# First attention layer of a two-layer hybrid model: the division of two softmaxes moved to TensorE and ScalarE, eight copies split by channel, one layer's order rewritten

## The chip, the core and the metric

One core of a Trainium2 chip runs the whole program in one launch. The metric is device time in microseconds. Engines are named as in the profile: PE (TensorE: matmuls and transposes into PSUM), DVE (VectorE), ACT (ScalarE), POOL (GpSimd) and SP (SyncE); the last two issue DMAs here. PSUM has eight banks, each as large as one 128 x 512 tile of 32-bit numbers.

## The reference, cut to what matters

Two kinds of layer alternate, A B A B, on `x` of 2048 tokens and 512 channels, each applied to the row-normalized `x` and added to it.

```
x = x + A(layernorm(x))     # long convolution: FFT, times the spectrum of K, inverse FFT; K from A, B, C, dt
x = x + B(layernorm(x))     # attention, 32 heads of 16, each token sees 8 keys at distances 0, 2, ... 14
x = x + A(layernorm(x))
x = x + B(layernorm(x))

def B(x):
    q, k, v = split(x @ wqkv)
    logits = q . k[pos - off] * scale         # masked where pos - off < 0
    attn = softmax(logits, over the 8 keys)
    o = sum over the 8 keys of attn * v[pos - off]
    return o @ wo
```

The softmax divides by its sum: exp(s (l - max)) / sum.

## The kernel before, in words

The convolution kernel's spectrum is made first (`kgen`), together with the first convolution. Then come the first attention layer, the second convolution (`a_layer`, order `CONV2`) and the second attention layer. Everything stays on the chip; the 16 token rows of a partition are grouped by four (`g` 0 to 3), so `Xg[g]` is 128 x 4 x 512.

An attention layer is written by `b_layer`. It registers small operations with a `Plan`: the engine (or a choice of engines, with an estimated time for each), the function that issues it, what it waits for, and which PSUM buffer it takes and drops. The text `LAYERS[layer]["order"]` then gives the order in which they are issued. A word names an operation: a block (for example `S20`), and a letter for its place in the block. A `+` behind a word takes the second engine of the choice (DVE, where the choice is ACT or DVE). Every engine works through its own instructions in that order. Times in the plan serve only to place filler matmuls on PE (`stream`); nothing in the finished program is scheduled by them.

The blocks of the layer are:

- `y0` to `y3`: last stage of the convolution before (PE), copied to `Xg` by ACT (L1532). `n0` to `n3`: statistics of a row (L1158, L1161, DVE), their logarithm and exponential (ACT), and the normalized row (L1174 on DVE or L1172 on ACT). `t0` to `t3`: transposes, copied by ACT and DVE (L1191).
- `K`, `Q`, `V`: projections (PE, L1205 and L1292), copied by ACT (L1208, L1299).
- `M0`, `M1`: nine DMAs each inside the value tile `V2` (L1316), that build the shifted copies; SP issues five, POOL four. They wait for all eight value copies of their half of the heads.
- `L`: products of queries with shifted keys (DVE, L1253 and L1255), summed by PE, copied to `Lsb` by ACT (L1280).
- `S i jh`: softmax of head group `i` (0 to 3) and half `jh` of the rows. Three DVE instructions find the maximum (L1336, L1342, L1344; one PE swap between them). For groups 0 and 1 DVE subtracts it (L1347) and ACT takes the exponential (L1348); for groups 2 and 3 (`pe_max`) PE subtracts it in PSUM and ACT takes the exponential from there (L1358). PE sums (L1369), ACT takes the logarithm of the sum (L1378) and the exponential of its negative (L1379, 128 columns), and DVE multiplies by it (L1380).
- `P`: attention times values (DVE, L1401), summed by PE (L1411), copied to `oT` by ACT (L1422).
- `R0` to `Rf`: output projection of one row plus `x` (PE, L1441, L1446), copied to `Xg` by ACT (L1469), for nine rows with a running sum for the next mean.
- `N0` to `N3`: normalization of the new `x`, and first stage of the next convolution. Each row gives two tiles, cosine (`r` = 0, from the pool `psA` of four banks) and sine (`r` = 1, from `psL` of two banks), and each tile is copied into `Z` by ACT or DVE (L1489). All 32 copies wait for `X`, the point at which the memory of queries and keys is free.

The second convolution starts with `T0` (L248): PE transposes of the first eight groups of channels in `Z`, into a bank of the space that `psA` had. A DVE copy (L254), a matmul (L263) and an ACT copy (L269) follow, and so on for sixteen such slices, each of which needs its own sixteenth of the channels from all 32 copies.

The functions that the change touches and what calls them:

Of the kernel before, what the change touches and what calls it, by code (L numbers as in the profile page):

```python
# [14 lines left out]
F32 = mybir.dt.float32  # L15
# [14 lines left out]
GE = 4  # L30
# [830 lines left out]
class Plan:  # L861
# [44 lines left out]
    def run(self, order):  # L906
# [16 lines left out]
        if todo:  # L923
# [15 lines left out]
    dict(order="y0a y0b y0c y0d n0a n0b n0c n0e n0d n0h n0g n0i n0f y3a y3b n3a n3c y1a y1b n3b n1a n0j n0k y1c y1d n1b n0l n0p+ n0o+ n0m+ n0n "  # L939
# [40 lines left out]
         third_norm=(),  # L980
         raw=[],
         y_add=[],
         pe_den=(),
         ot_any=[],
         thirds=[],
         stores=[]),
# [36 lines left out]
         kept=[],  # L1023
         third_norm=(),
         raw=[],
         y_add=[],
         pe_den=(),
         ot_any=[],
         thirds=[12, 13, 14, 15, 10, 11],
# [675 lines left out]
```

## Time and profile before

| what | value |
|---|---|
| timed runs | 423.75, 425.57, 426.43 us, median 425.57 |
| profiled execution | 423.79 us, its span 422.0 us |
| PE clock granted | 0.999 |
| DVE busy in the span | 399.5 us, 95% |
| ACT busy in the span | 329.4 us, 78% |
| first attention layer | 151 to 275.2 us of the span |
| second convolution, sixteen slices | 275.2 to some 303 us |
| second attention layer | from 303 us to the end |

In the tables by stretch, a row gives the stretch, its length, then busy time and count of instructions of PE, PE weight loads, DVE, ACT and POOL, the granted clock, the share of DMA time and GB/s. In the tables of groups, a row gives the code line, engine, operation, output and input with shapes and count, then the busy time of the group and the mean of one in ns, then the engine's idle time just ahead of the group and what ended it. In a timeline, start and length in us come first, and idle time stands in brackets.

### The profile page before, as it was taken

How to read it: one execution, taken by the hardware profiler on the slowest of the kernel's cores; microseconds unless marked ns; L12 is line 12 of the kernel's file. 1: busy time of each engine (PE TensorE's matmuls, PEld its weight loads, DVE VectorE, ACT ScalarE, POOL GpSimd, SP SyncE). 2: the span in 40 equal slices, each digit the busy share in tenths (PEclk: the TensorE clock that was granted, in tenths of full speed). 3: DMA queues.
4: the chain of work that ended last, by engine and by line, in shares of the span. 5: the costliest groups of instructions: out<-in, count | busy, mean ns of one | idle time of the engine just before them, and what ended most of it. 6: DMA issues, size and time to landing. Idle time of an engine off the chain costs nothing.

```text
span 422.0 us, 12184 instructions
## 1 busy us (share of the span) xinstructions
PE 373.6 (89%) x5071; PEld 257.2 (61%) x5112; DVE 399.5 (95%) x736; ACT 329.4 (78%) x598; POOL 26.0 (6%) x68
## 2 busy tenths in 40 slices
PE   1167998999989999999997899889999999996996
PEld 1033685676458755687865565368855686875563
DVE  5999999999889989899999999999989999999994
ACT  6999999998979989757655489989988676663542
POOL 5000011011210000002010000000000001200000
PEclk9999999999999999999999999999999999999999
DMA  8900001253889950006282062239300009360022
GB/s 239 427 28 0 3 13 46 76 167 102 253 245 273 275 193 3 2 2 123 55 168 59 2 196 57 99 102 294 109 0 4 2 2 168 63 124 2 26 78 101
DMA packets 25823, 44.09 MB, mean 104 GB/s; under 512 B 7318, under 2 KB 17239, under 8 KB 25127
## 3 DMA queue, kind: packets, MB, share of 16 engines
q1 hardware_dynamic: 22918, 38.09, 31.4%
q0 software_dynamic: 1888, 4.56, 5.0%
q8 instruction: 40, 0.66, 0.7%
q10 hardware_dynamic: 960, 0.66, 0.5%
q14 instruction: 17, 0.13, 0.1%
HBM read 29.04 MB, written 6.95 MB: 85 GB/s over the span
## 4 chain that ended last, share of the span: by engine, by line
PE 39%; DVE 27%; ACT 11%; issue 6%; DMA 5%; SPq 2%; DVEq 0%; ACTq 0%
DVE prodpv L1401 11%; PE ps_qk L1205 8%; DVE prodqk L1255 5%; PE vp L291 4%; PE ps_v L1292 4%; PE psg L601 3%; PE Lp L1277 3%; ACT Z L1489 2%; DVE Z L504 2%; PE psk L568 2%; DMA Kt<-kt_scratch 2%; DMA V<-V 2%; PE ps_y L344 2%; PE pt_x L1188 2%; ACT xc L269 2%
## 5 line engine op out<-in xcount | busy, mean ns | idle before, releaser
L1401 DVE TENSOR_TENSOR prodpv<-V,Lsb 128x2048 bf16<-128x2048 bf16 x64 | 75.3, 1218 | 0.1
L1205 PE MATMUL ps_qk<-xnT,wqk 128*128 128x512 bf16 x256 | 60.1, 379 | 0.0
L1253 DVE TENSOR_TENSOR prodqk<-qT,N 128x1024 bf16<-128x1024 bf16 (+3 forms) x88 | 42.5, 538 | 2.1 <-ACT N L1208 1.8
L1255 DVE TENSOR_TENSOR prodqk<-qT,N 128x1024 bf16<-128x1024 bf16 (+3 forms) x56 | 40.5, 762 | 0.2 <-ACT qT L1208 0.2
L1411 PEld LDWEIGHTS <-prodpv 128*128 128x128 bf16 x1024 | 34.3, 98 | 9.8 <-DVE prodpv L1401 4.1
L1411 PE MATMUL po<-halves,prodpv 128*128 128x64 bf16 x1024 | 37.3, 193 | 2.9 <-DVE prodpv L1401 2.9
L275 DVE TENSOR_TENSOR pab<-xc,Kt 128x2048 bf16<-128x2048 bf16 (+1 forms) x34 | 38.6, 1151 | 0.1
L1205 PEld LDWEIGHTS <-wqk 128*128 128x128 bf16 x256 | 23.6, 98 | 23.5 <-DVE xnT L1191 0.2
L269 ACT CAST xc<-xp 128x1024 bf16<-128x1024 f32 (+1 forms) x34 | 34.7, 1035 | 2.1 <-PE xp L263 1.2
L291 PEld LDWEIGHTS <-pab 128*128 128x128 bf16 x512 | 30.4, 98 | 6.3 <-DVE pab L275 2.8
L291 PE MATMUL vp<-sb_IC,pab 128*128 128x128 bf16 x512 | 33.3, 219 | 0.9 <-ACT VT L295 0.4
L295 ACT CAST VT<-vp 128x1024 bf16<-128x1024 f32 (+1 forms) x31 | 32.5, 1079 | 0.2 <-PE vp L291 0.2
L1441 PE MATMUL ps_o<-wo_t,oT 128*128 128x512 bf16 x122 | 31.9, 379 | 0.6
L1422 ACT CAST oT<-po 128x512 bf16<-128x512 f32 x32 | 17.7, 588 | 18.5 <-PE po L1411 18.4
L1277 PEld LDWEIGHTS <-prodqk 128*128 128x128 bf16 x1024 | 29.3, 96 | 4.5 <-DVE prodqk L1255 1.8
L1277 PE MATMUL Lp<-sb_bones,prodqk 128*128 128x8 bf16 x1024 | 30.2, 166 | 1.2 <-DVE prodqk L1255 1.1
L1292 PE MATMUL ps_v<-wv,xnT 128*128 128x256 bf16 x256 | 30.3, 272 | 0.0
L528 PE MATMUL psadd<-Z,sb_ident 128*128 128x512 bf16 (+3 forms) x72 | 18.5, 339 | 12.9 <-DVE Z L504 6.9
L1299 ACT CAST V<-ps_v 128x512 bf16<-128x512 f32 x32 | 18.6, 585 | 13.2 <-PE ps_v L1292 13.1
L1158 DVE BATCH_NORM_STATS2 ln_stats<-X 128x6 f32<-128x512 bf16 x39 | 24.8, 679 | 2.8 <-ACT X L1532 2.7
L1208 ACT CAST N<-ps_qk 128x512 bf16<-128x512 f32 x32 | 18.5, 590 | 10.5 <-PE ps_qk L1205 10.2
L1292 PEld LDWEIGHTS <-xnT 128*128 128x128 bf16 x256 | 24.3, 97 | 3.6
(197 smaller groups left out, 821.7 us busy)
## 6 DMA issues: line engine op xcount, KB each, us to landing
Kt<-kt_scratch SPq DMA_DIRECT2D x60, 256.0 KB
kt_scratch<-ks SPq DMA_DIRECT2D x32, 128.0 KB
G<-c_G SPq DMA_DIRECT2D x2, 1536.0 KB
V<-V SPq DMA_DIRECT2D x8, 288.0 KB
X<-in_A_u_dram SPq DMA_DIRECT2D x4, 512.0 KB
F1Tsb<-c_F1T SPq DMA_DIRECT2D x2, 1024.0 KB
V<-V SPq DMA_DIRECT2D x4, 512.0 KB
V<-V POOLq DMA_DIRECT2D x4, 384.0 KB, 8.3
```

What stands on the lines that cost most here:

```text
L269: nc.scalar.copy(xcs[cg][:, gs].rearrange("q g o l -> q (g o l)"), xps[cg][:].rearrange("q h n -> q (h n)")[:, gs.start * 128:gs.stop * 128])
L275: nc.vector.tensor_tensor(pabs[cg][:, gs], xcs[cg][:, gs].to_broadcast([128, gs.stop - gs.start, 2, 128]), kts[cg][:, gs], ALU.mult)
L291: a.last_pe = nc.tensor.matmul(vp[:, g, :], pabs[cg][:, gs.start + g, ab, :], C["IC"][:, ab, :], start=(ab == 0), stop=(ab == 1))
L295: copy(dst[..., parts(cg)[part]], vps.pop((cg, part))[:].rearrange("k g (q e) -> k q e g", e=GE))
L1205: nc.tensor.matmul(t.ps[:], wqk[:, ct, f0:f0 + 128], x_group(g)[:, :, ct], start=(ct == 0), stop=(ct == 3))
L1253: nc.vector.tensor_tensor(b.pr[:, u:u + 2 * n, 1 - halves_of[0], :], q, cols(kT[i][:, starts[0]:starts[0] + n * 128]), ALU.mult)
L1255: nc.vector.tensor_tensor(b.pr[:, u:u + 2 * n].rearrange("f u a q -> f a u q")[:, ::-1], q.unsqueeze(1).to_broadcast([128, 2, 2 * n, 64]), ...
L1277: nc.tensor.matmul(t.Lp[:, w, u % 2, u // 2, :], b.pr[:, u].rearrange("f a q -> f (a q)"), bones[:], start=False, stop=(t.parts == W // 2 ...
L1292: nc.tensor.matmul(t.ps[:, jj, :], tokens(ct, jp * 2 + jj, c), wv[:, ct, fp * 256:(fp + 1) * 256], start=(jj + ct == 0), stop=(jj == 1 and ...
L1401: nc.vector.tensor_tensor(t.p2[:, c:c + k, 0:nj, :].rearrange("p c j (d h) -> p c j d h", d=DH), m.V2[i // 2][:, c0 + c:c0 + c + k, r0:r0 ...
L1411: nc.tensor.matmul(po[jj // k][:, jj % k, c, :], t.p2[:, c - c0, jj, :], fold, start=(first and c == c0 and jj % k == 0), stop=(last and c ...
L1441: nc.tensor.matmul(t["ps"][:], m.oT[:, ft, j * 128:(j + 1) * 128], wo_t[:, ft, :], start=(start and ft == lo), stop=(ft == 3 or kept and f ...
```

## The change

In the first attention layer only:

1. `pe_den=(2, 3)`: for head groups 2 and 3 the first exponential goes to a tile of its own; ACT makes only the logarithm of the sum; PE builds the difference again, now with the logarithm subtracted as a third matmul; and a second exponential of 512 columns on ACT writes the finished weights. The multiply on DVE (L1380) and the 128-wide exponential (L1379) go, for four softmaxes.
2. `z_split`: for rows 8 to 11 (the group `N2`) each of the eight copies into `Z` becomes two, one for channels 0 to 255 and one for 256 to 511, each on either engine. The sine tiles of these rows are taken from `psO` (two banks) instead of `psL`.
3. The copy of an output row can go to DVE where no running sum is wanted.
4. A block `C` of operations that issue nothing stands for the first slice of the next convolution: its first step needs only the first halves, later ones the second halves as well.
5. A new order of the whole layer.

Counted by words and their marks, the new order differs from the old as follows (first attention layer, before and after):

| kind | DVE | ACT |
|---|---|---|
| normalized rows | 30 to 27 | 2 to 5 |
| whole copies into `Z` | 10 to 5 | 22 to 19 |
| halves: first, second | 0 to 4, 0 to 3 | 0 to 4, 0 to 5 |
| output rows | 0 to 2 (rows 11, 12) | 16 to 14 |
| softmax multiply, groups 2 and 3 | 4 to 0 | |

Three of the eight split tiles have one half on each engine. Behind the last first half stand two second halves on DVE and three on ACT. SP's moves of `M0` go in the order (numbers from 0) 2, 4, 6, 0, 8 instead of 0, 8, 4, 6, 2; number 0 is the largest. The first values used are those of head group 1 (`P10`) instead of group 0 (`P00`). Memory that the copies need is free (`X`) at word 526 of 734 instead of 552 of 713.

```diff
 LAYERS = (
-    dict(order="y0a y0b y0c y0d n0a n0b n0c n0e n0d n0h n0g n0i n0f y3a y3b n3a n3c y1a y1b n3b n1a n0j n0k y1c y1d n1b n0l n0p+ n0o+ n0m+ n0n "
...
-               "N2m N3m+ N3q N3r N3t N3w N1p N3E N3u N2n+ N2p+ N2C N2q+ N2o+ N3s+ N2A N2E N2y N2w N2s N2D N2G N2z+ N2x+ N2t+ N2F N2B N2H N2u N2v "
-               "N2r",
+    dict(order="y0a y0b y0c y0d n0a n0b n0c n0e n0d n0i n0f y1a y1b n1a n0h n0g y1c y1d n1b n1c y2a y3a n0j n0k y2b y3c n2a n1d n0l n1e n0p+ "
...
+               "N3B N3t N3C N3w N3s N3D N3u N2n+ N2s N3F N2q+ N2p+ N2o+ N2Q N2M N2t+ N2N+ N2O+ N3G+ N2I N2w N2u N3E N2A N2r N2P N2B+ N2y N2x N2z "
+               "N2R N2U N2V N2J N2v N2E N2F+ N2S+ N2W Ca Cb N2C+ N2K N2G Cc Cd Ce N2D N2X N2H N2L N2T",
...
-         pe_den=(),
+         z_split=[[8, 0], [8, 1], [9, 0], [9, 1], [10, 0], [10, 1], [11, 0], [11, 1]],
+         pe_den=(2, 3),
...
-            got["X", j] = plan.add("ACT", act_us(512) + 0.095 * (j % 4 in x_sums[j // 4] and not last_layer), evict, [p], drop=[alloc])
+            if j % 4 in x_sums[j // 4]:
+                got["X", j] = plan.add("ACT", act_us(512) + 0.095, evict, [p], drop=[alloc])
+                return
+            got["X", j] = plan.add(dict(ACT=act_us(512), DVE=0.61), None, evict, [p], drop=[alloc])
+
+        firsts, seconds = [], []
...
-                        t.ps = (m.psL if r else psA).tile([128, 512], F32, name="ps_s", tag="psL" if r else "psA")
+                        t.ps = dict(psA=psA, psL=m.psL, psO=m.psO)[t.pool].tile([128, 512], F32, name="ps_s", tag=t.pool)
...
-                    def evict(eng, jj=jj, r=r, t=t):
+                    def evict(eng, c0=0, c1=16, jj=jj, r=r, t=t):
                         (nc.scalar.copy if eng == "ACT" else nc.vector.tensor_copy)(
-                            z_view(m.Z)[:, r, 4 * g + jj], t.ps[:].rearrange("k (c e g) -> k c g e", c=16, e=GE))
-                    p = plan.add("PE", 0.22, pe, [normed[jj]], take=PL if r else PA)
-                    plan.add(dict(ACT=act_us(512), DVE=0.61), None, evict, [p, x_end], drop=[p])
+                            z_view(m.Z)[:, r, 4 * g + jj, c0:c1], t.ps[:, c0 * 32:c1 * 32].rearrange("k (c e g) -> k c g e", c=c1 - c0, e=GE))
+                    split = [4 * g + jj, r] in lay["z_split"]
+                    pool = PA if not r else PO if split else PL
+                    t.pool = pool[0]
+                    p = plan.add("PE", 0.22, pe, [normed[jj]], take=pool)
+                    if not split:
+                        firsts.append(plan.add(dict(ACT=act_us(512), DVE=0.61), None, evict, [p, x_end], drop=[p]))
+                        continue
+                    us = dict(ACT=act_us(256), DVE=0.34)
+                    halves_of = [plan.add(us, None, lambda eng, c0=c0, evict=evict: evict(eng, c0, c0 + 8), [p, x_end]) for c0 in (0, 8)]
+                    firsts.append(halves_of[0])
+                    seconds.append(halves_of[1])
+                    plan.add("-", 0.0, lambda: None, halves_of, drop=[p])
...
+        if not last_layer:
+            plan.block = "C"
+            p = plan.add("PE", 0.44, lambda: None, firsts, take=PA, cols=0)
+            plan.add("-", 0.0, lambda: None, [p], drop=[p])
+            o = plan.add("DVE", 0.6, lambda: None, [p] + seconds)
+            p = plan.add("PE", 0.43, lambda: None, [o], cols=0)
+            plan.add("ACT", 0.905, lambda: None, [p] + seconds)
```

More of the change, by code (lines that the diff above doesn't have):

```diff
@@ L1026 @@
          y_add=[],
+         z_split=[],
          pe_den=(),
```

50 rows, old and new, of the table LAYERS are left out of this document.

## The prediction

> **What bounds the kernel now.** I read the page first, then busy time by stage, then what VectorE (DVE) waited for, then the timeline around the end of the stage that the change rewrites. The page gives the span and the busiest engine:
>
> ```profile
> span 422.0 us, 12184 instructions
> PE 373.6 (89%) x5071; PEld 257.2 (61%) x5112; DVE 399.5 (95%) x736; ACT 329.4 (78%) x598; POOL 26.0 (6%) x68
> ```
>
> The whole change lies in the first attention layer, from 151 us (first output rows of the first convolution) to 275.2 us (last copy into `Z`). By stretch (columns: PE, weight loads, DVE, ACT, POOL):
>
> ```profile
> 151.00:275.20 124.20, 116.96 (x1570) 76.67 (x1576) 120.58 (x241) 91.26 (x197) 4.44 (x8) 1.00 0.28 71
> 215.00:235.00 20.00, 16.88 (x351) 12.54 (x352) 20.00 (x29) 10.42 (x24) 0.00 (x0) 1.00 0.43 93
> 235.00:255.00 20.00, 18.35 (x306) 12.22 (x308) 20.00 (x30) 14.91 (x42) 0.00 (x0) 1.00 0.35 107
> 255.00:275.20 20.20, 17.84 (x130) 8.02 (x130) 19.54 (x44) 20.07 (x50) 0.00 (x0) 1.00 0.24 79
> 240.50:275.20 34.70, 31.76 (x363) 17.29 (x364) 34.04 (x67) 33.04 (x87) 0.00 (x0) 1.00 0.34 107
> ```
>
> DVE works 120.58 of 124.20 us, so it idles 3.6 us, all of it near the two ends: from 215 to 255 it is full. In the last 20 us ACT is full too (20.07 of 20.20). DVE is the bound, and at the end DVE and ACT are bounds together. What DVE waited for in this stage and in the next convolution:
>
> ```profile
> DVE ln_stats L1158 <- ACT X L1532: 1.4, 1, 1.4
> DVE zt L254 <- PE pt L248: 1.1, 2, 0.8
> DVE prodqk L1253 <- ACT N L1208: 0.9, 1, 0.9
> DVE ln_nb L1166 <- ACT ln_rstd L1165: 0.6, 1, 0.6
> ```
>
> The border itself, by the timeline:
>
> ```profile
> 270.72 4.50 ACT L1489 CAST Z<-ps_s 128x512 bf16<-128x512 f32 x9
> ...
> 270.97 1.70 DVE L1174 TENSOR_SCALAR N<-X,ln_rstd,ln_nb 128x512 bf16<-128x512 bf16 x5
> ...
> 272.58 2.54 DVE L1489 CAST Z<-ps_s 128x512 bf16<-128x512 f32 x4
> ...
> 275.27 0.90 PEld L248 LDWEIGHTS <-Z 128*128 128x128 bf16 x16 [1.64 <-ACT Z L1489]
> ...
> 275.94 0.69 DVE L254 COPY zt<-pt 128x1024 bf16<-128x1024 bf16 x1 [0.81 <-PE pt L248]
> ```
>
> Both engines finish their copies at about 275.2; only then does PE transpose, and DVE stands 0.81 us. That hole is what the channel halves can fill.
>
> **The change part by part.** Prices are distances from start to start where operations follow each other, since they overlap by some 0.04 to 0.1 us. The rows:
>
> ```profile
> L1380 DVE TENSOR_TENSOR Lsb<-Lsb,sm_rdb 128x512 bf16<-128x512 bf16 x16 | 6.6, 417 | 0.0
> L538 ACT CAST Utab<-psadd 128x512 bf16<-128x512 f32 x8 | 4.5, 657 | 0.0
> L538 ACT CAST Utab<-psadd 128x256 bf16<-128x256 f32 x12 | 4.0, 390 | 0.7 <-PE psadd L528 0.6
> L1379 ACT ACTIVATE sm_rdb<-den 128x128 bf16<-128x128 f32 x16 | 4.3, 278 | 0.3
> L1172 ACT ACTIVATE N<-X,ln_nb,ln_rstd 128x512 bf16<-128x512 bf16 x4 | 3.3, 813 | 0.3 <-DVE ln_nb L1166 0.3
> ```
>
> ```profile
> 189.37 0.28 DVE L1344 TENSOR_TENSOR sm_mx<-sm_m,ps_max 128x128 bf16<-128x128 bf16 x1
> 189.57 1.22 DVE L1253 TENSOR_TENSOR prodqk<-qT,N 128x768 bf16<-128x768 bf16 x3
> ...
> 197.31 0.41 DVE L1380 TENSOR_TENSOR Lsb<-Lsb,sm_rdb 128x512 bf16<-128x512 bf16 x1
> 197.65 2.84 DVE L1255 TENSOR_TENSOR prodqk<-qT,N 128x1024 bf16<-128x1024 bf16 x4
> ...
> 207.23 4.62 DVE L1401 TENSOR_TENSOR prodpv<-V,Lsb 128x2048 bf16<-128x2048 bf16 x4
> ```
>
> *Softmax of heads 2 and 3* (four instances). DVE loses L1380: it starts at 197.31 and the next at 197.65, so 4 x 0.34 = -1.36 us. ACT loses the exponential of 128 columns (0.28) and gains one of 512 from PSUM, which I price like a 512-wide `Z` copy, 4.50 / 9 = 0.50: 4 x 0.22 = +0.9 us. PE gains three 512-wide matmuls each, 12 in all. PE holds 53.07 busy us in the 60.2 us from 215 on (16.88 + 18.35 + 17.84), and DVE never waits for it there, so I cost them at nothing. If a chain were uncovered, the product behind it would wait for about half a microsecond of ACT plus the matmuls.
>
> *Normalized rows.* Three go from DVE to ACT. DVE: 1.70 / 5 = 0.34 each, -1.02 us. ACT: 0.81 each, +2.4 us.
>
> *Output rows 11 and 12* are copied by DVE: 2 x (2.54 / 4 = 0.64) = +1.28 us on DVE, 2 x 0.50 = -1.0 us on ACT.
>
> *Copies into `Z`.* Whole ones: 10 to 5 on DVE (-3.2 us), 22 to 19 on ACT (-1.5 us). Halves: 7 on DVE and 9 on ACT. The trace has no 256-wide DVE copy from PSUM; between 0.20 (L1344, 128 wide, next start 0.20 later) and 0.64 (512 wide) a line through the two gives 0.35, so +2.45 us (bounds 1.4 and 4.5). On ACT the step from 512 to 256 in L538 is 0.27, so 0.23 at the least, 0.50 at the most; I take 0.27: +2.4 us.
>
> DVE in sum: -1.36 - 1.02 + 1.28 - 3.2 + 2.45 = **-1.85 us** (bounds -2.9 and +0.2). ACT in sum: +0.9 + 2.4 - 1.0 - 1.5 + 2.4 = +3.2 us.
>
> *The ACT load in the tail.* Behind the word of the first output row (row 7; its first weight load ran at 234.6) the new order has, by kind, +3.5 us on ACT: two softmax exponentials of 512 (+1.0), two normalized rows (+1.6), halves less whole copies (+0.9), two row copies less (-1.0), an `oT` and a projection copy more (+1.0). From 235 on ACT is free for 40.2 - 34.98 = 5.2 us (14.91 + 20.07 busy), but from 240.5 only for 1.66. Spread well, it costs nothing; squeezed behind 240.5 it costs 3.5 - 1.66 = 1.8. I take +0.6, nearer the first end, since 3.6 us of the free time lies just ahead of 240.5 and the new order opens `Z` earlier (526 of 734 words against 552 of 713).
>
> *The rotated values of heads 0 and 1* (nine moves inside `V2`, SP and POOL queues). Their present course:
>
> ```profile
> 192.01 0.58 ACT V L1299
> ...
> 193.97 2.48 SPq L1316
> ...
> 197.58 7.81 DMA V<-V
> ```
>
> ```profile
> L1253 DVE TENSOR_TENSOR prodqk<-qT,N 128x1024 bf16<-128x1024 bf16 x40 | 26.5, 684 | 2.1 <-ACT N L1208 1.8 <-ACT qT L1208 0.3
> ```
>
> The last value copy ends at 192.6, the last move lands at 205.4 (197.58 + 7.81), 12.8 us later; the first product (L1401) starts at 207.2, so the cover is 14.6 us, and DVE works through all of it. By counting words between those two points, the new order has there 18 query-key products instead of 23 (18,688 columns instead of 21,760) and one L1380 less. A product of 1024 columns takes 26.5 / 40 = 0.66 us, so 3,072 columns and one L1380 are 3 x 0.66 + 0.34 = 2.3 us. Cover 12.3 against 12.8: a wait of 0.5 us. SP's order changes as well: the largest move was issued first and now follows three smaller ones, and the five issues took from 192.6 or so to 197.58. Three fifths of these 5 us are 3.0. The ends are 0 (no wait) and +3.5 (0.5 + 3.0); I take +0.6, by the count. POOL's four moves keep their queue and stand behind the same value copies. The second set (heads 2 and 3) will have 8 products of L1401 (4.62 / 4 = 1.16) and 9 query-key products as cover, 8 x 1.16 + 9 x 0.66 = 15.2 us, above 12.8, so nothing.
>
> *The border.* With second halves behind the first ones, three ACT halves (3 x 0.27) and two DVE halves (2 x 0.35 = 0.7) run while PE makes the first transposes, in the hole of 0.81. Gain 0.7 at most. Against it: the last DVE half and the half-read tile of row 9 (cosine) share one `psA` buffer, and the first transposes need a bank of that pool; by counting the takes in the new order (109 in four buffers) the tile in the first bank is just that one, read out by DVE last. If buffers go round in turn the gain is nil. I take -0.5 of -0.8 to 0.
>
> Sum: -1.85 + 0.6 + 0.6 - 0.5 = **-1.15 us**. The profiled execution took 423.79 us (span 422.0), which would become 422.6. The three timed runs have the median 425.57, and with the profiled one the four mean 424.9, 1.1 above it. I put the sum to that mean: **423.7 us**.
>
> **The rivals.**
>
> *Two engines can't read one PSUM tile together.* Three of the eight split tiles have one half on DVE and one on ACT. The trace has such pairs in the first stage of the first convolution, where DVE takes one half of a tile and ACT the other:
>
> ```profile
> L641 DVE CAST Z<-ps_s 128x512 bf16<-128x512 f32 x8 | 5.4, 689 | 2.8 <-ACT Z L643 2.6
> ```
>
> ```profile
> 102.97 0.69 DVE L641 CAST Z<-ps_s 128x512 bf16<-128x512 f32 x1 [0.56 <-ACT Z L643]
> ```
>
> There DVE waited for ACT's half. Three such waits of a half's length (0.35) cost 1.0 us at the busiest place: 424.7. Against it: in the order the two halves of a mixed tile stand apart, with other copies between. The Trainium skill, page "PSUM — Partial Sum Buffer", section "PSUM bank collisions raise a hardware error", says that two engines must never touch one bank in the same partitions at once, reads included, so software has to make them take turns. By that rule all three pairs are serialized and 424.7 is the time; the trace agrees with it in L641's 2.6 us.
>
> *The bound's idle time goes as well.* A reordering could also remove DVE's waits at the head, 1.4 + 0.9 + 0.6 = 2.9 us. With neither the wait for the values nor the ACT term: -1.85 - 0.8 - 2.2 (three quarters of 2.9) = -4.85, or 420.0. For it: the head of the order is rewritten. Against it: the first 1.4 waits for the first output rows, before which DVE has nothing.
>
> *The values land late (slower).* If the largest move, now fourth, is held up by three issues and lands 3.0 us later, DVE waits 0.5 + 3.0 = 3.5 us at the first product: -1.85 + 3.5 + 0.6 - 0.5 = +1.75, or 426.7 from the mean. It decides the sign from a wait of 1.75 us on (1.85 + 0.5 - 0.6). Against it: nine moves share the DMA engines, so the last landing follows the bytes more than the order.
>
> *ACT bounds the tail.* At +1.8 instead of +0.6 the sum is +0.05: 425.0. For it, the 33.04 of 34.70; against it, two row copies leave ACT.
>
> **How the numbers follow.** Forecast (DVE relieved, a little of it given back) 0.48, its own range 422 to 425.3; idle time goes too 0.16; tiles read in turn 0.11; values late 0.15; ACT tail 0.10. Faster or slower by over 1% (4.2 us, about what a measurement of this kernel tells from no change) means below 420.7 or above 429.1. Below: most of the idle case, 0.12 in all. Above: values late together with DVE's upper bound, 0.07. The rest, 0.81, is within 1%. The range goes from the idle case, 420.0, to a little beyond the late values, 427.0.
>
> **What would show it.** DVE's busy time between the first output rows and the last `Z` copy: 118.7 instead of 120.6. L1380 with 12 instead of 16 instructions. No `DVEq` wait over 1 us ahead of the first L1401 (otherwise the values were late). ACT's free time behind the first output row down to about 2 us. At the border DVE's wait before the first `zt` copy below 0.3 instead of 0.81; if it is still 0.8, the transposes waited for a bank. The prediction is wrong if the time from the last `Z` copy to the end changes by more than 0.5 us, since nothing there was touched, or if the stage gets longer with DVE less busy.

## The result, and the profile after

The changed kernel takes 428.6 us, the median of 22 runs (424.91 to 430.95); the kernel before takes 425.64 us beside it (22 runs, 423.75 to 429.24). The ratio is 1.006, interval 1.0041 to 1.0079: slower by 0.6%, or 3.0 us, where 423.7 us was forecast. The profiled execution of the changed kernel took 425.87 us, less than most of its runs, and its span is 2.0 us longer than that of before.

The numbers of lines have moved: up to the copies of output rows they are those of before plus 2, the copy of a row is L1469 on DVE and L1471 on ACT, the copy into `Z` is L1496.

From the page:

```profile
span 424.0 us, 12243 instructions
PE 379.7 (90%) x5120; PEld 259.1 (61%) x5120; DVE 398.6 (94%) x733; ACT 333.0 (79%) x605; POOL 26.0 (6%) x68
```

The stage from the first output rows to the end of the last copy into `Z`, by stretch:

```profile
151.70:277.56 125.86, 121.00 (x1599) 78.90 (x1597) 119.46 (x238) 94.04 (x204) 4.50 (x8) 0.99 0.30 71
```

DVE works 119.46 us in it, 1.1 less than the 120.58 of before, and yet the stage has grown from 124.2 to 125.9 us. So DVE idles 6.4 us instead of 3.6. What it waited for there (engine and line, total, times, longest):

```profile
DVE ln_stats L1160 <- ACT X L1549: 1.4, 1, 1.4
DVE sm_mx L1346 <- PE ps_max L1342: 1.4, 2, 0.8
DVE xnT L1193 <- PE pt_x L1190: 1.2, 2, 0.8
...
DVE prodpv L1403 <- ACT Lsb L1360: 0.5, 1, 0.5
```

The border to the next convolution, by the timeline:

```profile
274.03 2.02 DVE L1496 CAST Z<-ps_s 128x256 bf16<-128x256 f32 x5
274.48 3.07 ACT L1496 CAST Z<-ps_s 128x256 bf16<-128x256 f32 x10 [0.37 <-DVE Z L1496]
...
275.95 0.38 PE L1493 MATMUL ps_s<-N,F1sb 128*128 128x512 bf16 x1 [0.39 <-ACT Z L1496]
276.36 1.09 DVE L1496 CAST Z<-ps_s 128x256 bf16<-128x256 f32 x3 [0.32 <-PE ps_s L1493]
276.90 0.85 PEld L248 LDWEIGHTS <-Z 128*128 128x128 bf16 x15 [1.62 <-ACT Z L1496]
...
277.58 0.69 DVE L254 COPY zt<-pt 128x1024 bf16<-128x1024 bf16 x1
```

The hole of 0.81 us is closed to 0.13 (276.36 + 1.09 to 277.58): the edit did here what it says. Just ahead of it stands a new wait of DVE, 0.32 us, for the last matmul of the first stage, which itself waited 0.39 us for ACT's copies. From the first `zt` copy to the end it takes 424.0 - 277.58 = 146.42 us, 146.06 before (422.0 - 275.94). The loss lies ahead of the border, and the waits of DVE for the maximum (`ps_max`) lead to it. The timeline of PE and DVE around the first of the two:

```profile
221.86 1.43 PE L1279 MATMUL Lp<-sb_bones,prodqk 128*128 128x8 bf16 x48
222.59 0.43 DVE L1382 TENSOR_TENSOR Lsb<-Lsb,sm_rdb 128x512 bf16<-128x512 bf16 x1
222.92 1.23 DVE L1403 TENSOR_TENSOR prodpv<-V,Lsb 128x2048 bf16<-128x2048 bf16 x1
223.15 0.63 PE L1413 MATMUL po<-halves,prodpv 128*128 128x64 bf16 x16
...
225.38 1.11 PE L1413 MATMUL po<-halves,prodpv 128*128 128x64 bf16 x32 [1.60 <-issue]
226.32 0.28 PE L1342 MATMUL ps_max<-sm_m,halves 128*128 128x128 bf16 x2
226.43 0.63 PE L1413 MATMUL po<-halves,prodpv 128*128 128x64 bf16 x16
226.63 0.48 DVE L1346 TENSOR_TENSOR sm_mx<-sm_m,ps_max 128x128 bf16<-128x128 bf16 x2 [0.54 <-PE ps_max L1342]
```

From 223.78 to 225.38 PE stands, and its wait is put down to "issue": nothing that the profile shows. No wait of that kind is among PE's of before. The second wait for `ps_max` follows a stretch at half the clock (columns as before, the granted clock third from the end):

```profile
243.00:244.00 1.00, 1.00 (x44) 1.00 (x41) 1.00 (x2) 0.39 (x3) 0.00 (x0) 1.00 0.00 0
244.00:245.00 1.00, 1.00 (x30) 1.00 (x27) 1.00 (x2) 1.00 (x3) 0.00 (x0) 0.67 0.00 0
245.00:246.00 1.00, 1.00 (x14) 0.72 (x12) 1.00 (x2) 0.94 (x4) 0.00 (x0) 0.50 0.00 0
246.00:247.00 1.00, 1.00 (x4) 0.29 (x2) 1.00 (x3) 0.97 (x3) 0.00 (x0) 0.50 0.00 0
247.00:248.00 1.00, 1.00 (x14) 0.59 (x13) 0.55 (x1) 0.04 (x1) 0.00 (x0) 0.62 0.00 0
```

PE counts as busy all through it, but from 244.3 to 247.7 it runs at 0.50, and DVE idles behind it (busy 0.55 of the last us). Each execution's mean clock gives an estimate of how many such stretches of 3.41 us it had (the share of the clock that is lost, times twice the span, over 3.41): on the mean of the timed ones 2.65 in the changed kernel, 0.8 to 1.3 in the kernel before, by group of runs. A line through span and number of stretches gives 0.6 to 1.4 us for each in most kernels here (1.7 to 2.4 in three).

### The profile page after: what moved, and what is told of

Its sections match the earlier page's. It is cut to its first block, busy times and chain, and to the rows that moved or that the text cites. A ratio compares the mean times of both kernels' runs of the same rounds, so it can differ in the third digit from the quotient of the medians.

```text
span 424.0 us, 12243 instructions
## 1 busy us (share of the span) xinstructions
PE 379.7 (90%) x5120; PEld 259.1 (61%) x5120; DVE 398.6 (94%) x733; ACT 333.0 (79%) x605; POOL 26.0 (6%) x68
## 4 chain that ended last, share of the span: by engine, by line
PE 50%; DVE 22%; ACT 8%; issue 5%; DMA 4%; SPq 1%; DVEq 0%; ACTq 0%
PE ps_qk L1207 12%; DVE prodpv L1403 7%; PE ps_v L1294 5%; PE Lp L1279 5%; DMA Kt<-kt_scratch 3%; PE vp L291 3%; PE psg L601 3%; DVE prodqk L1257 3%; DVE Z L504 2%; PE psk L568 2%; PE po L1413 2%; PE ps_o L1443 2%; DVE pab L275 2%; PE pt_x L1190 2%; PE ps_y L339 2%
## 5 line engine op out<-in xcount | busy, mean ns | idle before, releaser
L1413 PEld LDWEIGHTS <-prodpv 128*128 128x128 bf16 x1024 | 35.4, 99 | 10.9 <-issue 3.2
L1413 PE MATMUL po<-halves,prodpv 128*128 128x64 bf16 x1024 | 38.3, 194 | 3.1 <-issue 1.6
L1443 PE MATMUL ps_o<-wo_t,oT 128*128 128x512 bf16 x128 | 33.9, 387 | 0.1
L528 PE MATMUL psadd<-Z,sb_ident 128*128 128x384 bf16 (+3 forms) x75 | 19.3, 344 | 12.7 <-DVE Z L504 7.5
L1301 ACT CAST V<-ps_v 128x512 bf16<-128x512 f32 x32 | 18.5, 587 | 10.7 <-PE ps_v L1294 10.6
L1210 ACT CAST N<-ps_qk 128x512 bf16<-128x512 f32 x32 | 18.6, 588 | 10.1 <-PE ps_qk L1207 9.7
```

The source lines that it names most:

```text
L1413: nc.tensor.matmul(po[jj // k][:, jj % k, c, :], t.p2[:, c - c0, jj, :], fold, start=(first and c == c0 and jj % k == 0), stop=(last and c ...
L1443: nc.tensor.matmul(t["ps"][:], m.oT[:, ft, j * 128:(j + 1) * 128], wo_t[:, ft, :], start=(start and ft == lo), stop=(ft == 3 or kept and f ...
```

## The experiments

The experiments e1 to e16 come in four groups of four, each on a chip of its own, with its own runs of the kernel before beside it; ratios are to these. The theories: **G**, the stretches at half clock cost the time; **W**, the waits that the new order makes between the engines do; and, from the second group on, **C**, TensorE runs out of code. "New order" is the changed layer's order, "old" that of before.

### Parts of the change, and fillings

**e1.** Two zero matmuls of 256 or 192 columns in each of the narrow sums of logits of head groups 2 and 3, to lift the columns per window.

```
                     for u in range(16):
+                        if not last_layer and i in (2, 3) and u % 8 == 4:
+                            nc.tensor.matmul(t.Lp[:, :, 0, 0:j1, :], ident[:], zeros, start=False, stop=False)
                         nc.tensor.matmul(t.Lp[:, w, u % 2, u // 2, :], ...)
```

> The changed kernel with two filler matmuls (256 or 192 columns of zeros, added to the sum and so without effect) in each of the 16 query-key sums of head groups 2 and 3 of the first attention layer. Theory G (the clock gate: stretches of PE work in narrow matmuls let the granted clock fall to a half): these stretches, near 222 and 241 us in the changed kernel, get 500 more columns per sum; the first layer shows no half-clock stretch, mean clock 0.995 or more, time 422.5 to 425, below the kernel before. Theory W (the new order itself waits more: DVE on softmax chains and transposes): PE has 32 more matmuls and nothing gets better, 427 to 430.

Measured: 428.16 us (9 runs), ratio 1.0082 (1.0045 to 1.0118); 1.9 half-clock stretches instead of 2.65 (2.2 with one run of 435.59 us that the ratio leaves out). The profile has none in the first attention layer, and is no shorter; a stall of 1.1 us put down to "issue" at 224.7 is still there. Fewer stretches alone didn't bring the time back.

**e2.** Old order with the division moved to PE and ACT, whole copies. The last operation of the four softmaxes concerned stands one word behind the one ahead of it.

```
-         z_split=[[8, 0], [8, 1], ...],
+         z_split=[],
          pe_den=(2, 3),
```

> The old order and whole copies, with the softmax division of groups 2 and 3 on PE and ACT (four second exponentials right behind their logarithms). Theory G: the order of narrow matmuls is the old one and 12 wide matmuls come on top, clock as before, time 0.5 to 1.5 us below the kernel before. Theory W: the longer chain of these softmaxes shows as DVE waits, 1 to 3 us above the kernel before at the same clock.

Measured: 426.96 us (11 runs), ratio 1.0066 (1.0032 to 1.01). In the old order the division on PE and ACT doesn't pay.

**e3.** New order without it.

```
-         pe_den=(2, 3),
+         pe_den=(),
```

> The new order and the halves, with the old division (multiply on DVE). Theory G: 6,144 wide columns fewer in PE's thin stretches, so as many half-clock stretches or more: mean clock 0.99 or less, 428 to 431. Theory W: the softmax chain is short again, 425 to 427.

Measured: 433.12 us (6 runs), ratio 1.0198 (1.0159 to 1.0236). DVE's multiplies now wait 4.0 us for the 128-wide exponential, and "issue" holds PE for 3.5 us. Neither part alone beats the kernel before: the division in the old order is as slow as the whole change, and the new order without the division is slower still, for it is written for the division.

**e4.** The change with the eight copies whole, each where its first half stood.

```
-         z_split=[[8, 0], [8, 1], ...],
+         z_split=[],
...
-                    pool = PA if not r else PO if split else PL
+                    pool = PA if not r else PO if g == 2 and not last_layer else PL
```

> The new order with the eight tiles copied whole, each on the engine and at the place of its first half. Both theories: the hole of 0.8 us at the border comes back, 0.3 to 0.9 us above the changed kernel, same clock as the changed kernel. If the halves cost more than they bring, it is up to 1 us faster instead.

Measured: 428.55 us (12 runs), ratio 1.0056 (1.0023 to 1.0089), the same as with halves. No gain from the halves shows, and the two profiles take the same 70.04 us from the first product with values to the first `zt` copy.

### The code packet

The second fact of these four profiles was the stall: each has it, somewhere from 223 to 228 us, whatever the edit. Counted by TensorE's instructions, it stands in all four (and in the first profile) right behind the same one, the 5,040th of matmuls and weight loads, although e2 has another order than the rest. That is no wait of the program; it is a place in the code. The page's table of queues has a queue 8 of kind "instruction" with 40 packets of 16 KB, one per some 256 instructions of TensorE (10,240 in all). The queues in the stretch from POOL's first move of the second set up to the packet, and in the next 1.7 us (queue, packets, MB, share of the 16 DMA engines' time), in the changed kernel:

```profile
q1 hardware_dynamic: 342, 1.06, 55.8%
q0 software_dynamic: 205, 0.58, 33.2%
...
q1 hardware_dynamic: 67, 0.17, 60.8%
q8 instruction: 1, 0.02, 5.5%
q0 software_dynamic: 3, 0.00, 0.3%
```

The same in the kernel before, 210.7 to 218.9 us, and the next 1.5 us:

```profile
q1 hardware_dynamic: 220, 0.67, 43.3%
q0 software_dynamic: 207, 0.58, 34.1%
...
q1 hardware_dynamic: 77, 0.27, 92.4%
q8 instruction: 1, 0.02, 5.2%
q0 software_dynamic: 1, 0.00, 0.0%
```

Queue 0 holds POOL's moves, queue 1 SP's. In the changed kernel 547 packets of these two queues go ahead of the code, in the kernel before 427. The packet starts at 222.59 us there, 10.9 us behind POOL's first move; before, at 219.03, 8.3 behind it. It takes 0.9 to 1.6 us, and PE starts again 1.2 to 1.6 us after it ends, in all twelve profiles with a stall. What the change did to these queues is in its order of the second set `M1` (issuing words only; numbers as in the description of the change; SP's five, then POOL's four):

```
-  M1y M1s M1g M1a M1m   M1j M1d M1v M1p       SP 8 6 2 0 4   POOL 3 1 7 5
+  M1g M1a M1s M1y M1m   M1j M1v M1p M1d       SP 2 0 6 8 4   POOL 3 7 5 1
```

POOL's one large move (number 1, 48 lanes of 8 rows) went from second to last.

**e5, e6.** The changed kernel and the kernel before without the second set of moves.

```
-                    eng.dma_start(T[lanes[0], ...], T[lanes[1], ...])
+                    if fp == 0 or last_layer:
+                        eng.dma_start(T[lanes[0], ...], T[lanes[1], ...])
...
-                            m.V2[i // 2][...]
+                            m.V2[i // 2 if last_layer else 0][...]
```

> Changed kernel without the nine moves that build the rotated values of head groups 2 and 3 (these groups read the rotated values of groups 0 and 1 instead, so their results are wrong; the number of products, matmuls and copies is the same). A new theory C (code): TensorE runs out of instructions near 224 us, because its next 16 KB of code, an instruction packet on queue 8, starts only when most of the V<-V packets ahead of it have passed (222.59 us in the changed kernel, where TensorE then stands from 223.8 to 225.38 us without any wait that the trace shows). Without the moves the packet comes early, the stall of 1.6 us and the thin place at 224 us vanish, and the kernel gains 0.5 us of DVE's wait plus about 0.65 of a half-clock stretch of 0.8 to 1.2 us: 427.4, or 1.2 us below the changed kernel. Theory W (the loss is in the waits that the order itself makes): no stall is involved, unchanged at 428.6.

> Kernel before without the same nine moves (heads 2 and 3 read the rotated values of 0 and 1, their results are wrong). Theory C: the kernel before has no such stall near 224 us (its packet started at 219.03 us, in time), so it gains nothing: 425.6, ratio 1.000. If it gains as much as the changed kernel does, the moves cost both alike and the refill of code doesn't explain the difference between the two.

Measured: changed 424.25 us (12 runs), ratio 0.996 (0.9939 to 0.998); before 424.86 us (12 runs), 0.9996 (0.9973 to 1.0019). The moves cost the changed kernel 4.3 us (428.6 to 424.25), far more than the 1.2 expected of C, and the kernel before nothing that can be told. Without them the change is a gain over the kernel before as it is; over e6 it is 0.6 us by the medians and 0.996 / 0.9996 = 0.9964, or 1.5 us, by the ratios, whose intervals just meet. With the queues empty the packet comes at the 4,781st and the 4,743rd recorded instruction; in traces that lack as many records as these two (e7, e16), PE runs dry behind the 5,021st. So the packet comes with 240 to 280 of TensorE's instructions left when nothing holds it up, and these are its margin.

**e7.** The changed kernel with the second set in the old queue order (the "-" line above). **e8.** The same with 512, 144, 240 and 512 zero columns at the thin place near 243 us.

> Changed kernel with the second set of moves issued in the order of the kernel before (SP 8, 6, 2, 0, 4 instead of 2, 0, 6, 8, 4; POOL 3, 1, 7, 5 instead of 3, 7, 5, 1); results right. In the trace of before POOL's packets of that set ended by 218.8 us and the code packet started at 219.03, in the changed kernel they ended at 222.5 and the packet started at 222.59. Theory C: the packet starts some 3 us earlier, the stall near 224 us shrinks from 1.6 us to below 0.7, and the time falls by 0.5 to 1.2 us, to about 427.6. Theory W: 428.6. If the packet starts as late as before this edit, the order of the moves isn't what delays it.

> The same with four fillings of zero columns on TensorE (512 ahead of the second output row's matmuls, 144 and 240 between the narrow sums of the last logits, 512 ahead of the products behind them) at the thin place at 241 to 245 us; results right. Theory G (the half-clock stretches): fewer than about 3,100 columns in a window of 3.41 us halves the clock for the next; the fillings lift the least window near 243 us from 2,304 to above 3,300 columns, which takes away 0.55 of a stretch per run on the mean; together with the earlier code packet the half-clock stretches per run fall from 2.65 to about 1.3 and the time to 426.5. Theory W: 428.6 plus up to 0.5 for the fillings.

Measured: e7 424.91 us (12 runs), ratio 0.9977 (0.995 to 1.0004); packet 10.1 us behind POOL's first move, stall 0.7 us. e8 424.87 us (12 runs), ratio 0.9985 (0.9957 to 1.0014); packet at 8.2 us, no stall; 1.16 half-clock stretches against 1.63 in e7. Nine words in another order bring back 3.5 us (1.006 to 0.9977), and W falls as the main cause. The fillings take stretches away, and no time that shows.

**e9.** The reverse: the kernel before with the second set in the new queue order (the "+" line), nothing else.

> Kernel before with only the second set of moves in the changed kernel's queue order (SP 2, 0, 6, 8, 4; POOL 3, 7, 5, 1); results right. Theory C: TensorE's code packet near 219 us starts 1.5 to 3 us later. The kernel before had used 4,845 of TensorE's instructions when the packet started, the changed one 4,971, and stood dry some 40 instructions later; at about 55 instructions per us the kernel before has some 3 us in hand, so it stalls for at most 0.5 us: ratio 1.000 to 1.002. If it slows by 0.5% or more, the queue order costs the time by itself, whatever the rest of the order is.

Measured: 427.19 us (9 runs), ratio 1.0039 (1.0011 to 1.0066), 1.8 us slower. I had expected 0.002 at most, having allowed it 3 us in hand; it has less. Its timeline of PE, which in the kernel before has no such wait:

```profile
222.28 0.52 PE L1276 MATMUL Lp<-sb_bones,prodqk 128*128 128x8 bf16 x15
224.33 0.98 PE L1276 MATMUL Lp<-sb_bones,prodqk 128*128 128x8 bf16 x33 [1.53 <-issue]
```

And its clock behind that:

```profile
226.00:227.00 1.00, 1.00 (x4) 0.30 (x2) 0.58 (x3) 0.39 (x1) 0.00 (x0) 0.50 0.00 0
227.00:228.00 1.00, 1.00 (x19) 0.93 (x18) 1.00 (x2) 0.58 (x1) 0.00 (x0) 0.50 0.00 0
```

A stall leaves few columns in its window, and here PE then runs 3.41 us at half clock, so that one late packet of 16 KB costs more than its own 1.5 us. In six of the twelve profiles with a stall (e2, e3, e7, e9, e10, e14) half clock follows like this. In the other six it doesn't: in the first profile of the changed kernel it comes 19 us after the stall, and nothing ties it to the code packet.

**e10.** The changed kernel with both sets in the old queue order, the four fillings, and 1,024, 480 and 512 zero columns at the thin places of the second attention layer. **e11.** The same, copies whole. **e12.** The kernel before with the three fillings of the second layer and one of 288 columns near 244 us.

> Changed kernel with both sets of moves in the queue order of the kernel before, the four fillings near 243 us, and three in the second attention layer (1,024 columns ahead of one product's matmuls near 386 us, 480 and 512 near 400 us), where the windows of both kernels fall to 2,432 and 2,304 columns; results right. Theories C and G: no stall near 224 us, half-clock stretches per run down from 1.16 (the run with the four fillings alone) to below 0.5, at 1.3 us each: 424.0, 1.3 us below the kernel before. If the stretches fall and the time does not, the fillings cost as much as they save.

> The same with the eight copies whole instead of in channel halves (each at the place of its first half); results right. Prediction's step: the halves cover 0.7 of the border's hole of 0.81 us for 0.3 us more on DVE; in the runs so far whole copies were not slower. Theory that the halves gain: 0.3 to 0.5 us slower than with halves. Theory that they gain nothing: the same within 0.3.

> Kernel before with the three fillings of the second attention layer and one of 288 columns near 244 us; results right. Theory G: half-clock stretches per run fall from 1.28 to below 0.5 and the time by 0.8 to 1.0 us, to 424.4. If so, the changed kernel with the same treatment should still be some 0.5 to 1.4 us ahead of it, which is what its relieved VectorE is worth.

Measured: e10 424.69 us (12 runs), ratio 0.999 (0.9965 to 1.0015); e11 425.2 us (12 runs), 0.9998 (0.9973 to 1.0022); e12 425.16 us (12 runs), 0.9985 (0.9956 to 1.0013). None is told apart from the kernel before. In e12 the stretches do fall to 0.46, and little time with them. In e10 and e11 the profiles have the stall again, 1.6 and 1.4 us, packet at 11.4 and 10.5 us, in the old queue order, though POOL's last packet is through at 8.2 and 8.3: the order alone doesn't decide it. Halves against whole, 0.999 to 0.9998, are not told apart.

**e13, e14.** Only POOL's four moves of the second set in the old order; only SP's five. **e15.** The changed kernel once more, for a second profile. **e16.** e7 once more, likewise.

> Changed kernel with only POOL's four moves of the second set in the order of the kernel before (3, 1, 7, 5 instead of 3, 7, 5, 1); SP's stay as changed; results right. In nine traces so far the code packet never started before POOL's last packet of that set: 8.2 us behind POOL's first issue in the old order of both queues, 10.8 to 11.2 in the new one. Theory P (POOL's queue holds the code packet up): its last packet comes 8.2 us behind the issue again, the packet starts 8.2 to 11.4 us behind it, and the time is near that of both old orders, ratio 0.998. Theory S (SP's queue does): packet at 10.7 us or later, ratio 1.004 to 1.006.

> Changed kernel with only SP's five moves of the second set in the order of the kernel before (8, 6, 2, 0, 4 instead of 2, 0, 6, 8, 4); POOL's stay as changed; results right. Theory P: POOL's last packet still 10.8 us or more behind its first issue, code packet not before it, ratio 1.004 to 1.006. Theory S: packet from 8.2 us on, ratio 0.998.

> The changed kernel once more, for a second profile. Theory C: code packet 10.7 us or more behind POOL's first issue, a stall of TensorE of 1 to 2 us without a releaser near 224 us. If the packet comes at 9 us and there is no stall, the first profile was a chance and the theory falls.

> The changed kernel with both queues of the second set in the old order once more, for a second profile. Packet between 8.2 and 11.4 us behind POOL's first issue; the stall is below 0.7 us if it is below 10.1 (0.7 us at 10.11 in the first profile), and above if it is later. This tells whether the packet's time varies from run to run of one program.

Measured: e13 423.76 us (12 runs), ratio 0.9985 (0.9964 to 1.0006); POOL's last packet 8.4 us behind its first issue, code packet at 10.2, stall 0.2. e14 426.14 us (12 runs), ratio 1.0021 (0.9998 to 1.0044); POOL's last packet at 9.0, code packet at 11.1, stall 1.8. e15: one run of 424.79 us, packet at 9.0, no stall. e16: one run of 426.36 us, packet at 10.0, stall 0.8.

POOL's order makes most of the difference (changed kernel 1.006, e13 0.9985, with intervals apart; e13 and e14, side by side, are 2.4 us apart); SP's may make some (e14 lies between, and its interval meets both sides). Neither theory had e14 right: POOL's last packet is early in POOL's new order, and the code packet is late all the same. In e16 the stall is longer than the 0.7 us that I had expected below 10.1. And e15 breaks what I had written for it: the packet came ahead of POOL's last one (11.05 us), and the stall of the first profile is not in every execution of the program. PE at the same place in e15, without a stall:

```profile
222.58 1.35 PE L1279 MATMUL Lp<-sb_bones,prodqk 128*128 128x8 bf16 x48
223.79 1.76 PE L1413 MATMUL po<-halves,prodpv 128*128 128x64 bf16 x48
225.39 0.34 PE L1342 MATMUL ps_max<-sm_m,halves 128*128 128x128 bf16 x2
```

So theory C stands in a weaker form: the packet's time varies between executions of one program, and the queue order changes the odds that it comes too late. That the pace of TensorE's instructions does so too is argued; no run varies it alone. One rival is untested: e15 is the only run of the changed kernel beside these groups, and its 424.79 us, beside 424.78 of the kernel before, lies below all 22 of the result, so the chip may have a part in the odds. It can't be all of it, since e4, e9 and e14, on three chips, are slow or tend to be.

### What an execution costs with and without it

From thirteen profiles (e1 to e4 and e11 change more than the moves and the fillings; e11, whole copies with a stall of 1.4 and no stretch, takes 68.69): the code packet behind POOL's first move, the stall of PE, half-clock stretches between the first product with values and the first `zt` copy, and the time from the one to the other.

| kernel | packet, us | stall, us | half-clock stretches | first product to `zt`, us |
|---|---|---|---|---|
| before | 8.3 | 0 | 0 | 68.71 |
| before, filled (e12) | 9.1 | 0 | 0 | 68.70 |
| before, no second moves (e6) | | 0 | 0 | 68.72 |
| before, new queue order (e9) | 10.7 | 1.5 | 1 | 71.04 |
| changed, first profile | 10.9 | 1.6 | 1 | 70.04 |
| changed, second profile (e15) | 9.0 | 0 | 0 | 67.40 |
| no second moves (e5) | | 0 | 0 | 67.29 |
| old queue order, filled (e8) | 8.2 | 0 | 0 | 67.34 |
| POOL's order old (e13) | 10.2 | 0.2 | 0 | 67.43 |
| old queue order again (e16) | 10.0 | 0.8 | 1 | 69.20 |
| both sets old, filled (e10) | 11.4 | 1.6 | 1 | 70.26 |
| old queue order (e7) | 10.1 | 0.7 | 2 | 70.64 |
| SP's order old (e14) | 11.1 | 1.8 | 2 | 71.55 |

The two ends for the changed kernel as it is, first of e15 (with the start of the layer's statistics), then of the first profile:

```profile
155.14 2.58 DVE L1160 BATCH_NORM_STATS2 ln_stats<-X 128x6 f32<-128x512 bf16 x4 [1.37 <-ACT X L1549]
...
208.19 1.22 DVE L1403 TENSOR_TENSOR prodpv<-V,Lsb 128x2048 bf16<-128x2048 bf16 x1
...
275.59 0.69 DVE L254 COPY zt<-pt 128x1024 bf16<-128x1024 bf16 x1
```

```profile
207.54 3.50 DVE L1403 TENSOR_TENSOR prodpv<-V,Lsb 128x2048 bf16<-128x2048 bf16 x3
```

DVE's share of the two, first profile and e15:

```profile
207.54:277.58 70.04, 65.18 (x938) 41.57 (x937) 67.15 (x109) 53.32 (x130) 2.24 (x4) 0.98 0.35 88
208.19:275.59 67.40, 63.50 (x932) 40.98 (x938) 66.78 (x109) 53.29 (x130) 2.24 (x4) 1.00 0.38 92
```

So DVE idles 2.9 us in the first and 0.6 in the second. Of the 2.3 us between them, 1.0 stands behind the stall (0.54 for `ps_max`, 0.49 for `Lsb` at 231.35) and 1.1 behind the stretch at half clock (0.83 and 0.31).

Undisturbed, the changed stretch takes 67.3 to 67.4 us in four profiles, the old one 68.7 in three: 1.3 us less. In this table a stall of 0.7 us or more brings, with the half-clock stretches beside it, 1.8 to 4.2 us on top, more than the gain.

## Why the prediction was wrong, point by point

**DVE's sum was nearly right.** Forecast -1.85 us; measured to the end of the last copy it is -1.1 in the first profile (120.58 to 119.46) and -1.6 in e15, without a stall:

```profile
152.49:275.57 123.08, 119.07 (x1589) 78.18 (x1597) 119.02 (x238) 93.81 (x203) 4.50 (x8) 1.00 0.32 72
```

L1380, now L1382, has 12 instructions instead of 16, as said. A half costs more than the 0.35 taken: five in a row on DVE take 2.02 us from 274.03 on (border's timeline), so one starts 0.40 after the other, 0.35 us more for seven. The groups have them at 421 ns each, against 681 for a whole copy:

```profile
L1382 DVE TENSOR_TENSOR Lsb<-Lsb,sm_rdb 128x512 bf16<-128x512 bf16 x12 | 5.0, 421 | 0.0
L1496 DVE CAST Z<-ps_s 128x512 bf16<-128x512 f32 x5 | 3.3, 681 | 0.0
L1496 ACT CAST Z<-ps_s 128x256 bf16<-128x256 f32 x9 | 2.7, 427 | 0.4 <-DVE Z L1496 0.4
L1496 DVE CAST Z<-ps_s 128x256 bf16<-128x256 f32 x7 | 2.6, 421 | 0.3 <-PE ps_s L1493 0.3
```

**The border came out near the forecast**: -0.5 forecast; the hole shrinks by 0.68, and the new wait ahead of it takes 0.32 back, so -0.36 measured. The transposes waited for no bank that DVE reads last: their weight loads start at 276.90, while DVE copies until 277.45. Of the three mixed tiles one made ACT wait for DVE, 0.4 us in the third row. Whether that was free isn't plain: ACT then copies without a pause to the end, the last matmul of the first stage waits 0.39 us for it, and DVE 0.32 for that matmul (second to fourth row of the border's timeline); the trace reads as one chain, and no run takes it apart. The row that I had read for this rival, L641, doesn't bear on it: its tile is 128 x 1024 in 32 bits, as large as two banks, and each engine reads one half. The split tiles here are one bank each.

**The values came in time.** I took +0.6 for the first product; DVE starts it without a wait. The rival "values land late" is out.

**ACT's load in the tail** cost DVE no more than that 0.32 us in e15; I took +0.6. **Idle time at the head** didn't go: a wait for transposes (1.2 us) is new, and the one for the copies of the keys (`N` of L1208, now L1210) fell from 0.9 to 0.6. Both are read best where no stall disturbs, in the waits of DVE in e15, over the whole stage; those for `X`, `xnT` and `N` are at its head:

```profile
DVE ln_stats L1160 <- ACT X L1549: 1.4, 1, 1.4
DVE xnT L1193 <- PE pt_x L1190: 1.2, 2, 0.9
DVE prodqk L1255 <- ACT N L1210: 0.6, 1, 0.6
DVE Z L1496 <- PE ps_s L1493: 0.3, 1, 0.3
```

Without a stall all of this adds up to more than the sum of -1.15: from the first statistics to the `zt` copy e15 takes 275.59 - 155.14 = 120.45 us and the kernel before 275.94 - 153.65 = 122.29, 1.8 less, 1.3 of it from the first product on. The start of before:

```profile
153.65 2.58 DVE L1158 BATCH_NORM_STATS2 ln_stats<-X 128x6 f32<-128x512 bf16 x4 [1.37 <-ACT X L1532]
```

The mechanism that I priced is there, and it isn't what decides the median.

**The step that failed** is the one on the moves: of the first set, "POOL's four moves keep their queue and stand behind the same value copies", and of the second set, "above 12.8, so nothing". What the runs showed in its place: the second set's order costs the changed kernel 3.5 us (428.6 to 424.91 in e7) and the kernel before 1.8 (e9). I asked of the moves only when they land and who reads them. I compared the order of the first set and not that of the second, where POOL's large move had gone to the end, and never asked what else the DMA engines carry in those microseconds: TensorE's own code. The view that names it, the queue of kind "instruction", is on the page of the kernel before. "I cost them at nothing" of PE's added work has the same gap: I took PE's busy time for its reserve, while its reserve there is 240 to 280 instructions of code, and the columns by which a window stays above some 3,100.

Named among the signs that would refute it was "if the stage gets longer with DVE less busy"; that is what came. The forecast range ended at 427.0 because its slow end held one late transfer, and that one read by DVE.

**What stays open.** Between e5 and the changed kernel lie 4.3 us. The half-clock stretches, 2.65 against 1.05 at about 1 us, make some 1.6 of it. The stall of the one profile made DVE wait 1.0 more; if the rest is stalls, the timed runs must stall longer or oftener than the profiled ones, which they can't show. Why the packet comes at 9.0 us in one execution and at 10.9 in another, and what it waits for, isn't shown either. And whether an old queue order makes a version faster than the kernel before is not settled: e7, e8 and e13 are at 0.9977 to 0.9985, with intervals that include 1.

## What to carry to other kernels

Where DMAs are moved or put in another order, look at every queue that they share engines with, the instruction queue among them, and count how many instructions TensorE runs while they last: here 48 narrow matmuls, with a weight load each, took 1.43 us. A wait put down to "issue" on PE that stands behind the same instruction count in kernels of different order points to missing code, not to a wait of the program. Before an order is judged by one profile, take a second one: here the same program ran this stretch in 67.4 and in 70.0 us.

## What the runs showed of the hardware that was not expected

- **Code is refilled behind data.** TensorE's 16 KB packet came 240 to 280 instructions ahead of need with the queues empty, and as late as 12.6 us (e3) behind POOL's first move with the moves there, with stalls of 0.2 to 2.5 us in twelve of eighteen profiles. The Trainium skill, page "Runtime: NRT & Kernel Launch", section "Instruction fetch mechanics", says that code comes in blocks of 16 KiB or 256 instructions through a DMA queue of its own, and that crossing a block is "mostly hidden". The traces agree on the blocks; hidden it is not in those twelve, the changed kernel's first one with the DMA engines 89% taken ahead of the packet (55.8 and 33.2 above).
- **A busy PE can be throttled.** In the nine profiles with all matmul records, from 45 to 417 us, every window of 3.41 us, on the grid that the half-clock stretches lie on, with fewer than 2,950 moving columns was followed by 3.41 us at clock 0.50 (15 of them), and none with more than 3,150; between the two it went either way. At full clock a window has room for some 8,100 (a 512-wide matmul follows another by 0.215 us). The page "TensorE: Matmul & The Clock Gate" of the Trainium skill, section "Part 1: The HAM clock gate", has a free-running window of this length, and the grid's phase does differ from run to run here; it speaks of how busy PE was, and here PE was shown busy 100% in narrow matmuls of 8 and 64 columns.
